# Last-batch tokens by one-hot products, a weight split by way of PSUM, and bound scatters, in a clustered attention and mixture-of-experts kernel

## The chip, the core and the metric

The kernel runs on one core of a Trainium2 chip. A core has five engines with queues of their own: PE (TensorE) for matrix products, DVE (VectorE) and ACT (ScalarE) for elementwise work, POOL (GpSimd) for elementwise work on SBUF and for DMAs with computed row numbers, and SP (SyncE), which issues the other DMAs. Each engine works its queue in order. The metric is the device time of one execution in microseconds; the median of three runs is quoted, and single executions of this kernel lie between 809 and 814 us.

## The reference

There are two parts. The first is attention over 4 batches of 8 heads, 768 tokens, 64 features, masked by clusters: a query sees only the keys that are assigned to its own centroid.

```python
q_assign = argmax(einsum('bhsd,hcd->bhsc', q_n, c_n), -1)
k_assign = argmax(einsum('bhsd,hcd->bhsc', k_n, c_n), -1)
mask = q_assign[:, :, :, None] == k_assign[:, :, None, :]
scores = where(mask, scale * (q @ k.T), -1e9)
attn = softmax(scores); out = attn @ v
```

Its output, seen as 3072 tokens of 512 features, goes through a two-stage router (4 groups, then 4 experts of the group), and each token through its one expert:

```python
h = maximum(xg[mask_e] @ w1[g, e], 0.0)      # 512 -> 1024
ye = h @ w2[g, e]                            # 1024 -> 512
out[tok_idx] = (g_w * e_w)[:, None] * ye
```

All is FP32. The kernel keeps that accuracy by splitting each operand into a high and a low FP16 part and adding three products (high by high, high by low, low by high).

## The kernel before, in words

**Attention.** The loop in `attention` goes through 32 heads of nine *steps*; a step is one 512-column piece of fine scores. In a step PE makes the fine scores (L342, L343, two PSUM buffers `psf`), ACT the exponentials (L347), POOL the low part of the probabilities (L349; in the last two heads DVE does every second one), PE the products with V of five steps earlier (L366, L367), and, up to 18 steps ahead, the coarse scores (L302), whose row maxima DVE takes out of PSUM (L305). `beside` runs at the end of each step and starts what is due: jobs at a given step, and *turns*, of which one at most starts in a step, the lowest priority number first. What shares the two PSUM buffers `psm` takes turns. The splits of later q, k and v already go by way of PSUM (`halves`, L198 and L199): ACT writes a scaled half there, and DVE subtracts the high part from it.

The instructions are not queued in the order of the code. A scheduler with a time model of its own fixes the order for each engine: an instruction may be placed early, into a gap, where the model has its inputs ready, and the order in the code is only a priority. `tc.issue_after(x)` forbids what is written under it to stand ahead of `x` on `x`'s own engine.

**Router.** After every second head `logits` adds a quarter of a batch's router products. `decide` then finds group and expert of each of the batch's 768 tokens, and a slot in a table in DRAM: one row of token number and gate for each expert and slot. Six scatters from POOL (L668, 128 rows each) write a batch's rows. For the last batch `decide` runs after attention, with `early` set.

**The first expert.** After batch 2 (of 0 to 3) `first` (L772) picks the expert with most tokens so far, f0. It loads f0's w1 in four chunks (`load_chunk`, 512 KB each, into the four buffers of `stage`), splits them (`split_chunk`: ACT the high part, L758, DVE the low part with one operation on two SBUF operands, L761), waits for batch 2's scatters, reads f0's table rows (L809), loads the chunks of w2, gathers up to 288 of f0's tokens (L889) and transposes them into `xTA`.

**After attention.** `part_a` puts those 288 tokens through f0; it also splits w2 there, between the first four of the eight pieces of the first layer (`up`, L927 to L930). Beside it the last batch is decided and scattered. f0's tokens of the last batch have an own region of the table, up to 128 rows. `slots_b` reads that region (`tB`) and the start of all regions (`tb`); `slots_b2` turns `tB` into row numbers (L1002) and gathers the rows (`xB`); `slots` brings `tb` into the order in which the experts are worked, by small FP32 products with a permutation (L1073), and gathers the rows of the first of them; `tokens` transposes `xB` on PE (L899, L901). `SLB`, `SLOTS` and `SLT` give the points of `part_a` behind which these are written. Then `ranks` works f0's last tokens (k = -1) and the other 15 experts (k = 0 to 14), with their weights streamed through `stage`, 4 MB each, and the results scattered to the output (L988).

## Time and profile before

| | |
|---|---|
| median of the runs (lowest to highest) | 810.94 us (809.08 to 813.51) |
| time of the profiled execution | 810.6 us |
| its span, first to last instruction | 808.9 us |
| busy: PE, DVE, ACT, POOL | 738.6, 621.1, 460.0, 497.0 us |
| mean granted clock of PE | 0.963 |
| attention | to about 441 us |
| part A, last batch's decision, f0's last tokens | 441 to 493 us |
| the other experts | 493 to 795 us |

A row of a timeline gives start and duration in us, engine, line, operation, and the tile written and those read; in brackets is the idle time of the engine just before, and what ended it. A row of groups gives the count, the busy time in all, the mean duration in ns, and the idle time before them. A row of stages gives the length of the stretch, the busy time of each engine with the number of its instructions, the clock that PE was granted, the share of DMA and GB/s.

### The profile page before, as it was taken

Reading aid. Unit: us, or ns where it says so; the run is one execution under the profiler, and the core shown is the slowest. Engines: PE = TensorE matmul, PEld = TensorE weight load, DVE = VectorE, ACT = ScalarE, POOL = GpSimd, SP = SyncE. Lnnn points to the kernel's source line nnn. Section 1 sums busy time; section 2 is a strip of 40 time slices with the busy share of each in tenths; the row PEclk is TensorE's granted clock in tenths of the full one; section 3 lists DMA queues with packets and bytes.
Section 4 is the critical chain, followed back from the end, with each engine's and each line's share of the span. In section 5 each row is a group of like instructions: output and inputs, shape, how many; then the busy total and the mean of one; then the engine's idle time right before and its main releaser. Section 6 shows DMA issues by size and latency. Waiting matters only on the chain. (4 is left out here: it accounts for less than half of the span.)

```text
span 808.9 us, 26554 instructions
## 1 busy us (share of the span) xinstructions
PE 738.6 (91%) x11034; PEld 627.1 (78%) x11034; DVE 621.1 (77%) x1193; ACT 460.0 (57%) x893; POOL 497.0 (61%) x497
## 2 busy tenths in 40 slices
PE   5899999989999899997699868999999999999992
PEld 3677788768887688875588655788779999999991
DVE  6998879878798788988865645767589988887840
ACT  4567868658686587765366445435544454555431
POOL 9487787697877878769663424525556544654330
PEclk6899999999999999999799989999999999999996
DMA  8856435235343352223210287866687678888700
GB/s 235 210 155 154 127 100 163 77 90 146 103 138 101 90 144 67 68 74 106 92 41 4 80 296 254 260 215 216 220 262 246 225 246 261 263 274 270 234 30 18
DMA packets 80616, 128.54 MB, mean 159 GB/s; under 512 B 9011, under 2 KB 47411, under 8 KB 80488
## 3 DMA queue, kind: packets, MB, share of 16 engines
q1 hardware_dynamic: 74636, 113.12, 46.8%
q0 software_dynamic: 5696, 13.61, 4.7%
q8 instruction: 88, 1.44, 0.8%
q14 instruction: 40, 0.33, 0.1%
q10 hardware_dynamic: 156, 0.03, 0.0%
HBM read 93.47 MB, written 14.11 MB: 133 GB/s over the span
## 5 line engine op out<-in xcount | busy, mean ns | idle before, releaser
L349 POOL TENSOR_TENSOR pl<-p 128x512 f16<-128x512 f32 x278 | 288.6, 1054 | 98.2 <-ACT p L347 93.8
L305 DVE TENSOR_REDUCE mpart<-psc 128x1 f32<-128x512 f32 (+1 forms) x282 | 190.3, 684 | 47.1 <-PE psc L302 46.6
L347 ACT ACTIVATE p<-psf 128x512 f32<-128x512 f32 x288 | 169.3, 595 | 80.3 <-PE psf L343 72.2
L366 PE MATMUL pso<-V,pl 128*128 128x65 f16 x1152 | 164.0, 195 | 5.5 <-POOL pl L349 5.3
L366 PE MATMUL pso<-V,p 128*128 128x65 f16 x1152 | 164.6, 195 | 0.8 <-issue 0.6
L367 PE MATMUL pso<-V,p 128*128 128x64 f16 x1152 | 163.7, 193 | 0.0
L367 PE MATMUL pso<-V,pl 128*128 128x64 f16 x1152 | 163.7, 192 | 0.0
L342 PE MATMUL psf<-A 82*128 82x384 f16 (+2 forms) x576 | 144.9, 277 | 2.3 <-DMA A<-mr 0.9
L343 PE MATMUL psf<-B 128*128 128x384 f16 (+2 forms) x576 | 145.1, 277 | 0.0
L367 PEld LDWEIGHTS <-p 128*128 128x128 bf16 x1152 | 113.6, 99 | 22.2 <-issue 1.5
L366 PEld LDWEIGHTS <-p 128*128 128x128 bf16 x1152 | 113.2, 98 | 16.8 <-issue 8.9
L302 PE MATMUL psc<-A 80*128 80x512 f16 (+1 forms) x376 | 109.7, 333 | 15.7 <-DVE mpart L305 14.4
L366 PEld LDWEIGHTS <-pl 128*128 128x128 f16 x1152 | 112.3, 97 | 6.5 <-POOL pl L349 5.9
L367 PEld LDWEIGHTS <-pl 128*128 128x128 f16 x1152 | 113.8, 99 | 0.6 <-issue 0.3
L930 DVE SCALAR_TENSOR_TENSOR hl<-psh,hh 128x160 f16<-128x160 f32 (+14 forms) x136 | 50.1, 370 | 56.4 <-ACT hh L929 47.2
L929 ACT ACTIVATE hh<-psh 128x160 f16<-128x160 f32 (+14 forms) x136 | 46.1, 346 | 64.8 <-PE psh L927 63.7
L927 PE MATMUL psh<-xT,wh0a 128*128 128x288 f16 (+7 forms) x512 | 75.6, 256 | 0.9 <-issue 0.5
L988 POOL DMA_INDIRECT out_dram<-y,ri x32 | 38.9, 1215 | 60.3 <-ACT y L987 55.2
L927 PE MATMUL psh<-xT,wh0b 128*128 128x272 f16 (+6 forms) x448 | 65.2, 254 | 1.6 <-ACT xT L901 1.2
L343 PEld LDWEIGHTS <-B 128*128 128x128 f16 x576 | 56.9, 99 | 11.2 <-issue 3.0
L342 PEld LDWEIGHTS <-A 82*128 82x128 f16 x576 | 55.9, 98 | 12.3 <-DMA A<-mr 1.0
L927 PE MATMUL psh<-xT,wl0a 128*128 128x288 f16 (+7 forms) x256 | 64.4, 256 | 1.0 <-issue 1.0
(297 smaller groups left out, 1747.5 us busy)
## 6 DMA issues: line engine op xcount, KB each, us to landing
st<-w SPq DMA_DIRECT2D x128, 512.0 KB
B<-parts SPq DMA_DIRECT2D x64, 192.0 KB
kx<-kT SPq DMA_DIRECT2D x16, 384.0 KB
qx<-qT SPq DMA_DIRECT2D x16, 384.0 KB
vx<-vr SPq DMA_DIRECT2D x16, 384.0 KB
A<-parts SPq DMA_DIRECT2D x32, 192.0 KB
xbuf<-xs SPq DMA_DIRECT2D x4, 1536.0 KB
A<-mk SPq DMA_DIRECT2D x56, 24.0 KB
```

Source lines behind the costliest of these rows:

```text
L302: last["mm"] = nc.tensor.matmul(out=pc[:, off:off + k1 - k0], lhsT=QA[h % 8][0:80, c * P:(c + 1) * P], rhs=KA[h % 8][0:80, k0:k1], start=T ...
L305: nc.vector.tensor_reduce(out=(mp[:, 0, 0:1], mp[:, :, 1], mp[:, 1, 0:1])[i], in_=pc.rearrange("p (a x) -> p a x", a=n), axis=AX.X, op=ALU ...
L342: nc.tensor.matmul(out=o, lhsT=KA[h % 8][0:82, ks], rhs=QA[h % 8][0:82, q0:q1], start=True, stop=False)
L343: nc.tensor.matmul(out=o, lhsT=KBs[h][:, ks], rhs=QBs[h][:, q0:q1], start=False, stop=True)
L347: cfg["exp"] = nc.scalar.activation(out=p32, in_=pf, func=AF.Exp, scale=QK / (SQ * SQ))
L349: (nc.vector if u in (EARLY if h < 2 else DVE_LO[h % 8] if h < NH - 2 else DVE_END) else nc.gpsimd).tensor_tensor(out=pl, in0=p32, in1=ph, ...
L366: nc.tensor.matmul(out=O[:, col:col + 65], lhsT=p[:, bs], rhs=vh, start=c == 0 and q == 0 and i == 0, stop=False, skip_group_check=True)
L367: nc.tensor.matmul(out=O[:, col:col + 64], lhsT=p[:, bs], rhs=vl, start=False, stop=c == NCH - 1 and i == 1, skip_group_check=True)
L927: self.mm = nc.tensor.matmul(out=ph[:, 0:M], lhsT=w[:, k, fs], rhs=xT[:, a, k], start=i == 0, stop=i == 3 * KD - 1)
L929: nc.scalar.activation(out=hh[:, f], in_=ph[:, 0:M], func=AF.Relu)
L930: self.ev = nc.vector.scalar_tensor_tensor(out=hl[:, f], in0=ph[:, 0:M], scalar=0.0, in1=hh[:, f], op0=ALU.max, op1=ALU.subtract)
L988: d = nc.gpsimd.indirect_dma_start(out=self.out, out_offset=bass.IndirectOffsetOnAxis(ap=idc, axis=0), in_=y[0:n], in_offset=None, bounds_ ...
```

## The change

Five things are changed.

1. `split_beside` takes the place of `split_chunk` for f0's weights. ACT writes the high part as before; then, in two turns of a `psm` buffer, ACT writes a scaled half of the chunk (512 columns) into PSUM, and DVE subtracts the high part from it.
2. w2 of f0 is loaded and split in `first`, thus in attention, and no longer in `part_a`. The four loads stand together ahead of the table read. `FIRST`, the number of steps between chunks, is 2 instead of 4. The two tiles of split w2 come from the pool `wa`.
3. A scatter of batches 0 to 2 and the gathers of `first` are bound behind POOL's latest low part by `issue_after`.
4. f0's tokens of the last batch are not read back from DRAM. `slots_b` compares each token's slot with the slot numbers of f0's last region and so makes one-hot matrices, 128 tokens by 128 slots for each of six token tiles, in FP32 (in a buffer of `stage`) and in FP16. `tokens_b` multiplies the last batch's attention output, which is still in SBUF, by them: 2 parts x 4 feature blocks x 6 tiles = 48 products of 128 columns give the transposed tokens at once, and six FP32 products of 2 columns give token numbers and gates. `tB`, `slots_b2` and that gather are gone.
5. `SLOTS` is 11 and `SLT` 13, counted in a `part_a` of 16 pieces (8 of the first layer, 8 of the second); before it was 18 and 17 of 20.

```diff
-FIRST = 4
+FIRST = 2
...
+        if lo.ins.engine == ET.Pool:
+            cfg["lo"] = lo
...
-            d = self.last["p"] = nc.gpsimd.indirect_dma_start(
+            with self.tc.issue_after(self.cfg["lo"].ins) if self.apart and not early and "lo" in self.cfg else ExitStack():
+                d = self.last["p"] = nc.gpsimd.indirect_dma_start(
...
-    SLOTS = 18
-    SLB = 11
-    SLT = 17
+    SLOTS = 11
+    SLT = 13
...
+    def after(self):
+        return self.tc.issue_after(self.cfg["exp"].ins) if "exp" in self.cfg else ExitStack()
+
+    def split_beside(self, st, hi, lo, i, q):
+        nc = self.nc
+        h, l = (w[:, *self.part(i, q)] for w in (hi, lo))
+        with self.after():
+            nc.scalar.activation(out=h, in_=st, func=AF.Copy, scale=WS)
+        n = st.shape[1] // 2
+        for j in range(2):
+            yield PSM, 1, 1
+            rows = slice(j * n, j * n + n)
+            t = self.R.psm.tile([P, 512], F32, name="psm").rearrange("p (a b) -> p a b", a=n)
+            with self.after():
+                nc.scalar.activation(out=t, in_=st[:, rows], func=AF.Copy, scale=WS)
+            nc.vector.tensor_tensor(out=l[:, rows], in0=t, in1=h[:, rows], op=ALU.subtract)
...
             if q >= 2:
-                with after():
-                    self.split_chunk(chunks[q - 2], *self.WA, 0, q - 2, 0)
+                yield from self.split_beside(chunks[q - 2], *self.WA, 0, q - 2)
...
+        w2A = [self.load_chunk(1, self.f0, q) for q in range(4)]
+        self.WA += self.wtiles(self.wa, 1)
         while R.done < R.B - 2:
             yield
...
-            self.w2A.append(self.load_chunk(1, self.f0, t + 1))
...
             if rows:
-                self.gather(ids[0:n, t:t + 1], n, xgs[t], rows)
-            for _ in range(4):
-                yield
+                with self.tc.issue_after(self.cfg["lo"].ins) if "lo" in self.cfg else ExitStack():
+                    self.gather(ids[0:n, t:t + 1], n, xgs[t], rows)
+            yield from self.split_beside(w2A[t], *self.WA[2:4], 1, t)
+        for q in range(nt, 4):
+            yield from self.split_beside(w2A[q], *self.WA[2:4], 1, q)
...
     def part_a(self):
-        w2 = self.W[1][0]
-        self.WA += w2
-        run = self.ffn(self.xTA, self.CA, self.WA, *self.colsA)
-        for q in range(4):
-            next(run)
-            yield
-            with self.tc.issue_after(self.R.last["v"].ins), self.tc.issue_after(self.R.last["a"].ins):
-                self.split_chunk(self.w2A[q], *w2, 1, q, 0)
-            yield
-        yield from run
+        yield from self.ffn(self.xTA, self.CA, self.WA, *self.colsA)
...
     def slots_b(self):
-        tB = self.small("tB", [P, 2])
-        R.reads(nc.sync.dma_start(out=tB, in_=R.table[E * R.BS:E * R.BS + P]))
...
+        nc.gpsimd.iota(sl, [[1, P]], base=E * R.BS, channel_multiplier=0, allow_small_or_imprecise_dtypes=True)
...
+        for c in range(T):
+            nc.vector.tensor_scalar(out=o32[:, c], in0=sl, scalar1=R.rows[:, c:c + 1], scalar2=None, op0=ALU.is_equal)
+        nc.scalar.copy(out=self.o16, in_=o32)
...
-    def slots_b2(self):
-        with self.tc.issue_after(self.ev.ins):
-            self.idB, self.gB = self.columns([self.tB[:, 0:1], self.tB[:, 1:2]], [P, 1], "b")
-        self.xB = self.gather(self.idB, P)
+    def tokens_b(self):
...
+        for a in range(2):
+            ps = R.psm.tile([P, 512], F32, name="psm")
+            for k in range(R.KD):
+                for c in range(T):
+                    nc.tensor.matmul(out=ps[:, k * P:(k + 1) * P], lhsT=xs[:, c, a, k * P:(k + 1) * P], rhs=self.o16[:, c], start=c == 0, stop=c == T - 1)
+            (nc.scalar.copy if a else nc.vector.tensor_copy)(out=xT[:, a], in_=ps.rearrange("p (k x) -> p k x", x=P))
+        ps = R.psm.tile([P, 512], F32, name="psm")
+        for c in range(T):
+            nc.tensor.matmul(out=ps[:, 0:2], lhsT=self.o32[:, c], rhs=self.pb[:, c], start=c == 0, stop=c == T - 1)
...
-            if i == X.SLB:
-                X.slots_b2()
             if i == X.SLOTS:
                 X.slots()
             if i == X.SLT:
-                X.xTB = X.tokens([X.xB], P)
+                X.xTB = X.tokens_b()
```

More of the change, by code (lines that the diff above doesn't have):

```diff
@@ L348, in fine @@
         ph = p32.bitcast(BF16)[:, 1::2]
-        (nc.vector if u in (EARLY if h < 2 else DVE_LO[h % 8] if h < NH - 2 else DVE_END) else nc.gpsimd).tensor_tensor(out=pl, in0=p32, in1=ph, op=ALU.subtract)
+        lo = (nc.vector if u in (EARLY if h < 2 else DVE_LO[h % 8] if h < NH - 2 else DVE_END) else nc.gpsimd).tensor_tensor(out=pl, in0=p32, in1=ph, op=ALU.subtract)
+        if lo.ins.engine == ET.Pool:
+            cfg["lo"] = lo
         Ph[h, u], Pl[h, u] = ph, pl
@@ L487, in av_next @@
             last = b == B - 1 and hh == H - 1
+            if last:
+                cfg["xs"] = XSt[b]
             if hh == H - 1:
@@ L526, in __init__ @@
         self.sm = ctx.enter_context(tc.tile_pool(name="rsm", bufs=1))
-        self.ident = cfg["ident"]
+        self.ident, self.cfg = cfg["ident"], cfg
         KD = self.KD = wr.shape[1]
@@ L655, in decide @@
         nc.vector.tensor_tensor(out=ps, in0=ps, in1=oe.rearrange("p t g x -> p t (g x)"), op=ALU.mult)
-        ds_ = sm.tile([P, T], F32, name="rds")
+        ds_ = self.rows = sm.tile([P, T], F32, name="rds")
         nc.vector.tensor_reduce(out=ds_, in_=ps, axis=AX.X, op=ALU.add)
@@ L667, in decide @@
                 yield
-            d = self.last["p"] = nc.gpsimd.indirect_dma_start(
-                out=self.table, out_offset=bass.IndirectOffsetOnAxis(ap=di[:, c:c + 1], axis=0),
-                in_=self.pay[:, t0 + c], in_offset=None)
+            with self.tc.issue_after(self.cfg["lo"].ins) if self.apart and not early and "lo" in self.cfg else ExitStack():
+                d = self.last["p"] = nc.gpsimd.indirect_dma_start(
+                    out=self.table, out_offset=bass.IndirectOffsetOnAxis(ap=di[:, c:c + 1], axis=0),
+                    in_=self.pay[:, t0 + c], in_offset=None)
             if self.apart:
@@ L789, in first @@
         self.WA = self.wtiles(self.wa, 0)
-        after = lambda: self.tc.issue_after(self.cfg["exp"].ins) if "exp" in self.cfg else ExitStack()
         chunks = []
@@ L809, in first @@
             R.reads(nc.sync.dma_start(out=tab[0:n, t], in_=tv[t * P:t * P + n]))
-        self.w2A = [self.load_chunk(1, self.f0, 0)]
-        for _ in range(FIRST):
+        for _ in range(FIRST + 1):
             yield
@@ L833, in first @@
             yield PSM, 2, 2
-            with after():
+            with self.after():
                 self.transposed(self.xTA, xgs[t], t, n, R.psm.tile([P, 512], F32, name="psm"))
@@ L843, in open @@
         wp = ctx.enter_context(tc.tile_pool(name="wp", bufs=1))
-        self.W = [[self.wtiles(wp, i, n) for n in "ab"] for i in range(2)]
+        self.W = [[self.wtiles(wp, 0, n) for n in "ab"], [self.WA[2:4], self.wtiles(wp, 1, "b")]]
         self.xp = ctx.enter_context(tc.tile_pool(name="mxp", bufs=2))
@@ L1053, in slots_b @@
         nc, R, E = self.nc, self.R, self.R.E
-        tB = self.small("tB", [P, 2])
-        R.reads(nc.sync.dma_start(out=tB, in_=R.table[E * R.BS:E * R.BS + P]))
-        self.tB = tB
+        T = R.rows.shape[1]
+        sl = self.small("sl", [P, P])
+        nc.gpsimd.iota(sl, [[1, P]], base=E * R.BS, channel_multiplier=0, allow_small_or_imprecise_dtypes=True)
+        t0 = R.N // P - T
+        pb = self.small("pb", [P, T, 2])
+        nc.vector.tensor_scalar(out=pb[:, :, 0], in0=R.pay[:, t0:t0 + T, 0], scalar1=-float(R.N), scalar2=None, op0=ALU.add)
+        nc.vector.tensor_copy(out=pb[:, :, 1], in_=R.pay[:, t0:t0 + T, 1])
+        o32 = self.stage.tile([P, 2, 512], F32, name="st").rearrange("p a b -> p (a b)")[:, 0:T * P].rearrange("p (c x) -> p c x", x=P)
+        self.o16 = self.small("o16", [P, T, P], F16)
+        for c in range(T):
+            nc.vector.tensor_scalar(out=o32[:, c], in0=sl, scalar1=R.rows[:, c:c + 1], scalar2=None, op0=ALU.is_equal)
+        nc.scalar.copy(out=self.o16, in_=o32)
+        self.o32, self.pb = o32, pb
         nt = self.nt = -(-max(self.caps) // P)
@@ L1059, in slots_b @@
         R.reads(nc.sync.dma_start(out=self.tb, in_=R.table.rearrange("(e s) w -> e s w", s=R.BS)[0:E, 0:nt * P]))
-    def slots_b2(self):
-        with self.tc.issue_after(self.ev.ins):
-            self.idB, self.gB = self.columns([self.tB[:, 0:1], self.tB[:, 1:2]], [P, 1], "b")
-        self.xB = self.gather(self.idB, P)
+    def tokens_b(self):
+        nc, R = self.nc, self.R
+        T = R.rows.shape[1]
+        xs = self.cfg["xs"]
+        xT = self.xp.tile([P, 2, R.KD, P], F16, name="xT")
+        for a in range(2):
[7 more added lines that the diff above has]
+            nc.tensor.matmul(out=ps[:, 0:2], lhsT=self.o32[:, c], rhs=self.pb[:, c], start=c == 0, stop=c == T - 1)
+        self.idB = self.small("bi", [P, 1], I32)
+        self.gB = self.small("bg", [P, 1])
+        nc.vector.tensor_scalar(out=self.idB, in0=ps[:, 0:1], scalar1=float(R.N), scalar2=None, op0=ALU.add)
+        nc.vector.tensor_scalar(out=self.gB, in0=ps[:, 1:2], scalar1=1.0 / (XS * WS * WS), scalar2=None, op0=ALU.mult)
+        return xT
     def slots(self):
```

## The prediction

> **What bounds the kernel now.** I read the stages first: PE's busy time and granted clock in stretches of the span.
>
> ```profile
> core 0: us, PE busy (x) PEld busy (x) DVE busy (x) ACT busy (x) POOL busy (x), PEclk, DMA share, GB/s
> 300.00:340.00 40.00, 39.73 (x775) 33.15 (x775) 33.58 (x72) 28.27 (x57) 31.80 (x32) 1.00 0.25 62
> 380.00:400.00 20.00, 12.58 (x208) 10.06 (x205) 17.05 (x21) 8.65 (x15) 15.30 (x15) 0.83 0.27 81
> 400.00:420.00 20.00, 16.98 (x285) 13.80 (x285) 15.84 (x27) 10.13 (x18) 12.43 (x13) 0.83 0.18 55
> 440.00:460.00 20.00, 17.61 (x208) 13.46 (x206) 14.96 (x50) 9.01 (x17) 7.04 (x6) 1.00 0.23 81
> 460.00:480.00 20.00, 13.22 (x92) 9.95 (x92) 5.84 (x11) 5.91 (x9) 3.52 (x5) 0.83 0.68 237
> 480.00:500.00 20.00, 16.41 (x187) 12.42 (x186) 10.31 (x21) 12.77 (x24) 13.62 (x12) 0.91 0.79 271
> 500.00:600.00 100.00, 100.00 (x864) 78.50 (x863) 73.63 (x112) 44.25 (x82) 44.71 (x36) 1.00 0.72 229
> ```
>
> PE is the bound nearly everywhere (39.73 of 40 us in steady attention, 100 of 100 in the ranks). So time is to be had only where PE stands still: 10.4 us in 380 to 420, and 2.4 + 6.8 + 3.6 = 12.8 us in 440 to 500. The other experts' stage has no idle PE; whatever comes earlier ahead of it, comes off the end.
>
> The first hole, from the timeline (start, duration) and windows of 5 us:
>
> ```profile
> 375.56 9.02 POOL L349 TENSOR_TENSOR pl<-p 128x512 f16<-128x512 f32 x9
> 379.14 6.52 DVE L761 SCALAR_TENSOR_TENSOR wl<-st,wh 128x1024 f16<-128x1024 f32 x1
> 386.78 0.58 PE L302 MATMUL psc<-A 80*128 80x256 f16 x2 [5.49 <-DVE mpart L305]
> 402.92 0.58 PE L302 MATMUL psc<-A 80*128 80x512 f16 x1 [4.85 <-DVE mpart L305]
> 451.19 1.23 DVE L761 SCALAR_TENSOR_TENSOR wl1a<-st,wh1a 128x1024 f16<-128x1024 f32 x1
> 451.44 1.88 POOL L668 DMA_INDIRECT table<-pay,rdi  x1 [12.07 <-DVE rdi L659]
> 385.00:390.00 5.00, 3.22 (x37) 2.47 (x37) 3.89 (x13) 0.82 (x2) 1.20 (x2) 0.51 0.35 105
> 400.00:405.00 5.00, 2.08 (x21) 1.56 (x21) 4.70 (x7) 0.00 (x0) 1.17 (x2) 0.52 0.31 95
> 405.00:410.00 5.00, 5.00 (x82) 4.13 (x80) 3.69 (x4) 3.48 (x6) 2.92 (x3) 0.80 0.04 13
> L761 DVE SCALAR_TENSOR_TENSOR wl<-st,wh 128x1024 f16<-128x1024 f32 x4 | 15.8, 3938 | 0.8 <-ACT wh L758 0.7
> ```
>
> The low part of a weight chunk takes DVE 1.23 us where POOL is in DMA work (451), and 6.52 us where POOL runs nine low parts in a row: that one ends at 385.66, about 1.1 us after POOL's row of 375.56 + 9.02 = 384.58. DVE waits for POOL here; behind it wait the row maxima, and behind these PE, 5.49 and 4.85 us. Then PE runs at half clock for a while: 3.22 x 0.49 + 2.08 x 0.48 + 5.00 x 0.20 = 3.6 us more.
>
> **The change, part by part.** (1) *Splits of w1.* DVE's one operation with two SBUF operands becomes two subtractions whose first operand ACT has put into PSUM. The kernel has such pairs already, 384 columns wide:
>
> ```profile
> L199 DVE TENSOR_TENSOR parts<-psm,parts x48: 543/551/559, 61.8 to 334.5; 128x384 f16<-128x384 f32 x48
> L198 ACT ACTIVATE psm<-vx 128x384 f32<-128x384 f32 x24 | 11.8, 490 | 3.9 <-DVE V L199 3.9
> L347 ACT ACTIVATE p<-psf 128x512 f32<-128x512 f32 x288 | 169.3, 595 | 80.3 <-PE psf L343 72.2 <-PE psc L302 6.6
> L758 ACT ACTIVATE wh<-st 128x1024 f16<-128x1024 f32 x4 | 4.2, 1056 | 0.0
> ```
>
> The first row decides: 48 subtractions with a PSUM operand, in attention beside a POOL that is 80% busy, none over 559 ns. So the holes of 10.4 us and the 3.6 us of slow clock behind them should go: **-14.0**. (The Trainium skill, SBUF — State Buffer, Who interferes with whom, says that of a DVE operation with two SBUF inputs and a GpSimd operation that reads SBUF the later one waits until the first finishes. By that rule a split loses at most one POOL operation, about 1 us, so the four would give 4 and not 14; the trace has a wait behind several in a row and 5.49 us on PE, and the trace decides.)
>
> At 512 columns a subtraction takes at most 551 x 512 / 384 = 735 ns, so DVE pays 8 x 0.7 = 5.9 us for w1 where it paid 15.8. It stays below PE.
>
> (2) *Splits of w2, moved from the first expert's products into attention.* Each split costs ACT 1.06 + 2 x 0.60 = 2.25 us. New on ACT are four high parts and 16 copies: 4 x 1.06 + 16 x 0.60 = 13.8 us; new on DVE for w2 5.9. Following the loop's turns in the code, one step being one 512-column piece of the fine scores: w1 falls on steps 243 to 261, w2 on 266 to 277 (scores end at 287). ACT over the 19 steps of w1: 19 x 0.60 + 4 x 2.25 + two router copies of 768 columns, between the 512 and the 1024 column rows, at 0.8 + two finishing casts of 384 columns at 0.49 = 23.0, and small ones; PE has, by 31 such pieces in its 40 us of steady attention less the q, k and v work that has ended, about 1.2 us a step: 23. Over w2's 12 steps: 7.2 + 9.0 + 1.6 + 0.5 = 18.3, while PE, whose coarse scores end at step 269, has about 4 x 1.2 + 8 x 1.0 = 13. ACT is the later one there by some 5, less one step that two score buffers cover. With 0.1 to 0.2 us of bank exchange a piece (3.9 us of idle in 24 pieces of the L198 row, and others have less) I take **+6.5**. Bounds: 0 if ACT's idle time takes all of it, +13.8 if all of it lies on the path. The w2 loads go to SP four at a time at step 263, behind w1's last split and ahead of the table read; a chunk has 3 steps before its split, and SP's next row-maximum transfer has 6 before its use: nothing, up to +2.
>
> (3) *Scatters of batches 0 to 2, and the first gathers, bound behind POOL's latest low part.*
>
> ```profile
> 163.55 1.20 POOL L668 DMA_INDIRECT table<-pay,rdi  x1 [0.33 <-DMA qx<-qT]
> ...
> 173.02 0.96 POOL L668 DMA_INDIRECT table<-pay,rdi  x1 [0.30 <-issue]
> PE pso L366 <- POOL pl L349: 2.5, 2, 2.2
> PE pso L366 <- POOL pl L349: 2.8, 2, 2.2
> 370.57 1.63 DVE L786 TENSOR_TENSOR cb<-cb,ft 128x16 f32<-128x16 f32 x1
> ```
>
> Six scatters stand in 10.5 us of POOL with only three low parts between them, so they were issued far ahead of their place in the code (every 5 steps, 4 for batch 2): 7.3 us of scatters in 8 to 9 steps, and PE waits 2.5 us (140 to 200) and 2.8 (245 to 300). Spread over 25 steps POOL, with 1.05 of about 1.3 us, works most of that off between them; I leave 0.4 each: **-4.5**. In batch 2 the crowded POOL also holds up small DVE operations (1.63 us for 16 columns); I count **-1**. Bounds 0 to -7.5. The price: batch 2's last scatter stands at step 262 and no longer ahead of it, so the table read of the first expert comes up to 15 steps later; its ids are wanted at 266 and may keep DVE waiting for 1 us, its rows at 279, which leaves a dozen us. The transposes fall on 279, 283, 286 (now 281, 286, 289), so part A isn't later: nothing, up to +2.
>
> (4) *The end of attention.* Waits of PE from 440 to 505, then the timeline:
>
> ```profile
> PE psm L899 <- DMA xg<-xbuf,bi: 4.6, 1, 4.6
> ...
> PE psh L927 <- DVE hl L930: 1.8, 2, 1.3
> PE psm L899 <- DMA xg<-xbuf,ri: 1.0, 1, 1.0
> 441.62 0.41 PE L927 MATMUL psh<-xTA,wh 128*128 128x288 f16 x2
> 459.44 0.96 POOL L668 DMA_INDIRECT table<-pay,rdi  x1 [0.30 <-issue]
> 465.89 0.15 DVE L1002 CAST bi<-tB 128x1 int32<-128x1 f32 x1 [5.32 <-DMA tB<-table]
> 466.53 1.14 PE L945 MATMUL psy<-hh,wh1a 128*128 128x288 f16 x8 [2.07 <-DVE yl L949]
> 466.93 0.99 POOL L889 DMA_INDIRECT xg<-xbuf,bi  x1 [4.39 <-issue]
> 474.21 1.03 PE L899 MATMUL psm<-ident,xg 128*128 128x128 f16 x8 [4.58 <-DMA xg<-xbuf,bi]
> 478.05 1.85 PE L1073 MATMUL psm<-perm,tb 16*128 16x16 f32 x12
> 493.25 0.41 PE L927 MATMUL psh<-xT,wh0a 128*128 128x288 f16 x2 [0.51 <-issue]
> ```
>
> The last batch's tokens go scatter, table, DVE, gather (7.3 us from 466.93 to PE), transposes. With the one-hot products the waits of 4.6 and of 2.1 (DVE stuck on the table) go, the rank's gather wait of 1.0 and the 1.3 on hl too, the latter since four wl1a of 1.23 leave DVE: 9.0. The slow clock goes: 13.22 x 0.17 + 16.41 x 0.09 = 3.7. Added on PE: 48 products of 128 columns at 0.06 (eight such take 1.03 at half clock) 2.7, six of FP32 at 0.15 (twelve in 1.85) 0.9, less eight transposes 0.5: +3.1. DVE's six comparisons of 128 columns (above the 0.15 of one column, below the 0.55 of 384) and ACT's 768-column copy lie beside part A's products, the slot numbers in POOL's 12.07 us of idle before its first scatter. One wait can take the old one's place: the expert permutation now comes after the second of four output blocks. PE gets there about 441.6 + 11.7 (96 of 0.122, by eight in 1.14) + 5.9 + 2 router + 1 = 462; scatters without DVE's four splits end near 458.5 instead of 460.4, and the table lands 5.5 us after that as now (460.4 to 465.9), at 464: 2 us, bounds 0 to 6. Sum -9.0 - 3.7 + 3.1 + 2 = **-7.6**, bounds -13 to 0. The rank's rows then have till 485 to arrive; gathered from 467 on, with the 7.3 us of the crowded one, they are there at 478. One of four staging buffers is held by the one-hot until then: covered by the five others.
>
> Sum: -14.0 + 6.5 - 5.5 - 7.6 = -20.6. From the profiled execution's 810.6 us (span 808.9, 1.7 around it) that is **790 us**; the median shown, 810.9, is 0.3 above that execution.
>
> **The rivals.**
> *ACT has room and PE finds the table there.* The L347 row's 80 us of idle ACT speaks for it, the count of step 266 to 277 against. The 6.5 falls to 1 and the 2 to 0, the scatters give all 7.5: 781.
> *The permutation waits like the old gather.* The weight stream starts ahead of the table read or the scatters stay slow; PE stands 6 us or more and slows its clock: (4) gives nothing, 798. For it: tokens were placed before their data now, too (4.58 us). (The Trainium skill, TensorE: Matmul & The Clock Gate, What's actually happening, has the clock fall to half after an idle window of about 3.4 us; the 0.51 after the 5.49 us wait agrees, and a 6 us wait would bring it again.)
> *The splits don't do what they say:* the new subtractions wait for POOL as the old did. Then -14 is lost: 804. The 559 ns maximum speaks against.
> *Slower: ACT and the two psm banks.* In the crowded steps each of the 24 pieces holds back the next exponential for its length and a wait for its bank, which DVE frees only after row maxima that wait for PE. Break-even is 20.6 + 6.5 = 27 us over eight splits, 3.4 us a split, 1.1 above its 2.25. At 4.4 a split: 35, so 819. For it: ACT falls behind PE at w2's steps. Against: 0.16 us of wait a piece in the L198 row.
>
> **How the numbers follow.** Forecast 790 (784 to 796): 0.53. 781: 0.15. 798: 0.17. 804: 0.03. Both the 798 case and all of ACT's 13.8 on the path, 805 to 812: 0.05. 819: 0.07. Under 0.5% (4 us) this kernel's change can't be told from none. Faster is the first four, 0.88; same 0.05; slower 0.07. From 777 to 805 the range leaves out the last two and a little below.
>
> **What would show it.** L761 in attention gone, no PE wait over 2 us on mpart, clock 1.0 from 380 to 420 (else 1 is wrong). Steps 266 to 277 with ACT near full and PE waiting on p (2). No wait of PE on pl near 170 and 270 (3). No PE wait on a gather for B, one under 3 us at the permutation, rank 0's first product 7 to 8 us sooner after part A's start than 51.6 (4). An unchanged ranks stage. A time over 805 would say that ACT, or the wait at the permutation, took what DVE gave.

## The result, and the profile after

The changed kernel takes 783.26 us (median; 782.34 to 784.30), the kernel before 810.91 us (809.08 to 813.51): a ratio of 0.9657, 95% interval 0.9628 to 0.9686. The forecast was 790 us, in a range of 777 to 805. The profiled execution after took 782.34 us, with a span of 780.6 us (before 808.9) at a mean granted clock of 0.978 (before 0.963). Two executions in the series below took far longer than all others of their kernel (2536.98 us of the kernel before, 1047.63 us of binding and split together), and the ratios leave them out.

The stages after, with the columns of the prediction's first fence:

```profile
380.00:400.00 20.00, 18.94 (x352) 15.49 (x350) 16.22 (x40) 16.07 (x30) 19.23 (x20) 1.00 0.25 68
400.00:420.00 20.00, 19.20 (x417) 16.93 (x415) 14.18 (x29) 17.21 (x33) 9.86 (x10) 1.00 0.05 16
440.00:460.00 20.00, 17.95 (x157) 14.44 (x157) 7.59 (x13) 5.71 (x8) 7.32 (x7) 0.91 0.74 247
460.00:480.00 20.00, 19.20 (x216) 14.74 (x214) 12.40 (x22) 14.66 (x28) 7.57 (x7) 1.00 0.82 280
480.00:500.00 20.00, 20.00 (x180) 16.17 (x178) 17.25 (x22) 8.93 (x19) 11.41 (x9) 1.00 0.83 258
```

PE is busy 38.1 of the 40 us from 380 to 420, where it had 29.6 at a clock of 0.83, and the clock there is now 1.00. ACT, 8.65 and 10.13 before, stands at 16.07 and 17.21 of 20.

The new splits on DVE and ACT (count, then shortest, median and longest in ns, first and last start), and the waits of PE from 140 to 200 us:

```profile
L784 DVE TENSOR_TENSOR wl<-psm,wh x16: 669/691/692, 366.2 to 408.9; 128x512 f16<-128x512 f32 x16
L783 ACT ACTIVATE psm<-st x16: 573/605/632, 365.6 to 408.2; 128x512 f32<-128x512 f32 x16
```

```profile
PE psm L651 <- DVE roe L639: 1.3, 1, 1.3
PE psc L302 <- DVE mpart L305: 0.2, 1, 0.2
```

Sixteen subtractions from PSUM, none over 692 ns, stand in place of eight operations on two SBUF operands, of which one took 6.52 us. And the wait of PE on `pl`, 2.5 us before, is gone. The timeline of POOL beside it, and then that of the end of attention (PE and SP's queue):

```profile
168.00 1.19 POOL L674 DMA_INDIRECT table<-pay,rdi  x1 [0.18 <-issue]
169.22 5.02 POOL L349 TENSOR_TENSOR pl<-p 128x512 f16<-128x512 f32 x5
174.41 0.99 POOL L674 DMA_INDIRECT table<-pay,rdi  x1 [0.17 <-issue]
...
421.10 0.41 PE L950 MATMUL psh<-xTA,wh 128*128 128x288 f16 x2
435.83 0.01 SPq L756 DMA_DIRECT2D st<-w  x1
437.52 0.96 POOL L674 DMA_INDIRECT table<-pay,rdi  x1 [0.30 <-issue]
443.92 0.35 SPq L1084 DMA_DIRECT2D tb<-table  x1
445.98 1.23 PE L1114 MATMUL psm<-perm,tb 16*128 16x16 f32 x9 [1.65 <-DMA tb<-table]
469.66 0.41 PE L950 MATMUL psh<-xT,wh0a 128*128 128x288 f16 x2
487.45 0.53 PE L950 MATMUL psh<-xT,wh0b 128*128 128x272 f16 x2
```

A scatter now comes every 6 to 7 us with five low parts between. Part A begins at 421.10 where it began at 441.62, which is 20.5 us earlier. Rank 1's first product comes at 487.45 where it came at 513.93, 26.5 us earlier; the remaining 1.8 of the span's 28.3 us lie in the ranks, where the profiles of this study differ by 3 us among themselves (292.7 to 295.9).

**Where the time came from.** The time at which a head is finished is the start of DVE's row that takes its denominators out of PSUM. After:

```profile
354.69 0.15 DVE L382 TENSOR_SCALAR DEN<-pso 128x6 f32<-128x6 f32 x1
392.21 0.16 DVE L382 TENSOR_SCALAR DEN<-pso 128x6 f32<-128x6 f32 x1
421.30 0.17 DVE L382 TENSOR_SCALAR DEN<-pso 128x6 f32<-128x6 f32 x1 [1.63 <-PE pso L369]
```

These are heads 25, 28 and 31; before, the same rows stood at 364.67, 414.70 and 441.81. The table gives, for every profile of this study, how much later (+) or earlier (-) than before each stage was passed, and last how long it takes from part A's first product to rank 1's. Heads 9 to 25 hold the scatters of batches 0 and 1, heads 25 to 28 w1's splits and the scatters of batch 2, heads 28 to 31 w2's splits where attention has them. What lies ahead of head 9 is start-up, which differs from execution to execution; it is in no stage.

| kernel | to head 9 | 9 to 25 | 25 to 28 | 28 to 31 | A to rank 1 |
|---|---|---|---|---|---|
| before | 0 | 0 | 0 | 0 | 72.31 |
| changed | -0.12 | -9.86 | -12.51 | +1.98 | 66.35 |
| changed, second profile | -0.36 | -10.02 | -13.80 | +2.76 | 68.38 |
| before, scatters bound | +0.43 | -9.94 | -3.92 | +1.32 | 72.05 |
| before, w1 split by PSUM | +0.35 | -1.28 | -10.30 | 0.00 | 68.23 |
| before, both of these | +2.37 | -9.96 | -13.79 | +2.95 | 67.36 |
| changed, scatters not bound | +2.87 | +1.86 | -9.80 | +0.75 | 67.02 |
| changed, split in SBUF | +0.32 | -9.96 | -10.77 | +4.91 | 66.88 |
| changed, scatters one step apart | +0.11 | -5.85 | -13.35 | +2.75 | 68.16 |
| changed, w2 split in part A | -0.54 | -9.99 | -12.53 | +0.04 | 71.03 |
| changed, table and gather | +0.27 | -9.86 | -13.66 | +2.99 | 69.87 |
| changed, w2's copies by VectorE | +0.27 | -10.02 | -13.75 | +5.50 | 64.91 |
| changed, permutation a step later | +1.26 | -10.05 | -13.61 | +2.76 | 65.72 |
| changed, w2's splits later | -0.33 | -10.03 | -13.72 | +2.49 | 66.35 |

### The profile page after: what moved, and what is told of

The parts are those of the page before. It is cut to its first block, busy times and chain, and to the rows that moved or that the text cites. A ratio compares the mean times of both kernels' runs of the same rounds, so it can differ in the third digit from the quotient of the medians.

```text
span 780.6 us, 26678 instructions
## 1 busy us (share of the span) xinstructions
PE 733.3 (94%) x11086; PEld 626.5 (80%) x11086; DVE 612.0 (78%) x1209; ACT 466.8 (60%) x910; POOL 495.6 (63%) x497
## 3 DMA queue, kind: packets, MB, share of 16 engines
q0 software_dynamic: 5616, 13.35, 4.9%
## 5 line engine op out<-in xcount | busy, mean ns | idle before, releaser
L368 PE MATMUL pso<-V,p 128*128 128x65 f16 x1152 | 161.6, 193 | 0.0
L368 PE MATMUL pso<-V,pl 128*128 128x65 f16 x1152 | 161.2, 194 | 0.0
L369 PE MATMUL pso<-V,pl 128*128 128x64 f16 x1152 | 161.0, 191 | 0.0
L369 PE MATMUL pso<-V,p 128*128 128x64 f16 x1152 | 160.8, 191 | 0.0
L952 ACT ACTIVATE hh<-psh 128x160 f16<-128x160 f32 (+14 forms) x136 | 46.6, 347 | 65.7 <-PE psh L950 64.3
L912 POOL DMA_INDIRECT xg<-xbuf,ri x32 | 43.5, 1359 | 39.8 <-PE psm L922 25.7
```

Of the source, the lines that this page charges most:

```text
L368: nc.tensor.matmul(out=O[:, col:col + 65], lhsT=p[:, bs], rhs=vh, start=c == 0 and q == 0 and i == 0, stop=False, skip_group_check=True)
L369: nc.tensor.matmul(out=O[:, col:col + 64], lhsT=p[:, bs], rhs=vl, start=False, stop=c == NCH - 1 and i == 1, skip_group_check=True)
L912: self.got = nc.gpsimd.indirect_dma_start(out=xg[0:n].rearrange("p a d -> p (a d)"), out_offset=None, in_offset=bass.IndirectOffsetOnAxis( ...
L952: nc.scalar.activation(out=hh[:, f], in_=ph[:, 0:M], func=AF.Relu)
```

## The experiments

The theory after the two traces: the scatters are worth about 10 us and not 5.5, because each wait on `pl` is followed by half clock, and the splits less than 14. The rivals are the prediction's own terms. "Before" and "changed" are the two kernels of this case; ratios are to the kernel before, run on the same chip (medians of 810.50, 807.58 and 809.15 us there), and the changed kernel has 0.9657 and, a second time, 0.9715. The same kernel's ratio thus moved by 0.6%, some 5 us, from one series to another; smaller differences between series are read from the stages.

### Binding alone, and the changed kernel without it

The kernel before, with only this (`lo` is kept as in the changed kernel):

```diff
-            d = self.last["p"] = nc.gpsimd.indirect_dma_start(
+            with self.tc.issue_after(self.cfg["lo"].ins) if self.apart and not early and "lo" in self.cfg else ExitStack():
+                d = self.last["p"] = nc.gpsimd.indirect_dma_start(
```

> The kernel before, with its scatters of batches 0 to 2 bound behind POOL's latest low part and nothing else changed. Theory A (the binding is worth what heads 10 to 19 show between the two traces, 5.1 + 4.7 us, because each crowd of scatters costs PE its wait and as much again at half clock; and DVE's long waits at the w1 splits come from POOL's backlog behind batch 2's scatters, so they shrink to about one POOL operation): 811 - 10 - (8 to 12) = 789 to 793, no PE wait over 2 us on the row maxima. Theory B (the binding is worth 10, but DVE's split waits as long as POOL has any low part to run, crowd or not): 801, with both PE waits of about 5 us still there. The prediction's own term (no slow clock): 805.5.

Measured: 796.97 us (796.26 to 799.12), ratio 0.9835 (0.9817 to 0.9852): 13.4 us from one small edit, between the two expectations and far over the prediction's term. Batches 0 and 1 gave 9.9 us; another 3.9 came in heads 25 to 28, where DVE still splits in SBUF. DVE and POOL there, then PE's waits from 360 to 415 us:

```profile
383.21 5.02 DVE L765 SCALAR_TENSOR_TENSOR wl<-st,wh 128x1024 f16<-128x1024 f32 x1 [0.73 <-issue]
383.11 4.02 POOL L349 TENSOR_TENSOR pl<-p 128x512 f16<-128x512 f32 x4
387.30 1.78 POOL L672 DMA_INDIRECT table<-pay,rdi  x1 [0.17 <-issue]
```

```profile
PE psc L302 <- DVE mpart L305: 7.6, 3, 3.9
```

In the kernel before, from 360 to 425 us:

```profile
PE psc L302 <- DVE mpart L305: 12.8, 4, 5.5
```

POOL's rows are four low parts long instead of nine, and DVE's operation still waits for a whole row: begun at 383.21 beside a row that ends at 387.13, it ends at 388.23. So binding also shortens PE's waits behind the splits, from 12.8 us in four to 7.6 in three, of which 3.9 is the longest. Neither theory's sign came: one wanted no wait over 2 us, the other both waits of about 5.

The other way round, the changed kernel with the scatters as before:

```diff
-            with self.tc.issue_after(self.cfg["lo"].ins) if self.apart and not early and "lo" in self.cfg else ExitStack():
-                d = self.last["p"] = nc.gpsimd.indirect_dma_start(
+            d = self.last["p"] = nc.gpsimd.indirect_dma_start(
```

> The changed kernel with its scatters free to be placed early again; the gathers stay bound. The binding as the two traces show it: 783.3 + 10 = 793, PE waiting on pl 2 to 3 us near 170 and 270 and at half clock after it. The prediction's term: 783.3 + 5.5 = 789. If the scatters only matter together with the old splits: 783.

Measured: 798.64 us (793.87 to 801.97), ratio 0.9839 (0.9800 to 0.9878), slower than all three expectations. Its profile spent 3 us more on start-up than that of the changed kernel; the stages say 11.7 us in heads 9 to 25 and 2.7 in heads 25 to 28. PE's waits from 140 to 200 us in it, and the stages behind them:

```profile
PE pso L368 <- POOL pl L349: 2.8, 2, 2.2
```

```profile
176.00:178.00 2.00, 0.03 (x1) 0.03 (x2) 1.32 (x3) 0.94 (x2) 1.97 (x3) 0.90 0.03 3
178.00:180.00 2.00, 2.00 (x20) 1.46 (x21) 0.00 (x0) 0.25 (x1) 2.00 (x3) 0.50 0.00 0
180.00:182.00 2.00, 2.00 (x48) 1.72 (x47) 1.21 (x2) 0.98 (x2) 2.00 (x3) 0.50 0.00 1
182.00:184.00 2.00, 2.00 (x30) 1.63 (x27) 1.48 (x3) 1.57 (x3) 1.93 (x3) 0.50 0.03 8
```

The wait of 2.2 us is followed by six us at half clock, which are 3 us more. In the kernel before the same wait was followed by less: by the rows of 174 to 180 us shown at the end, 0.88 x 0.28 + 2.00 x 0.50 + 2.00 x 0.08 = 1.4 us more. This slow clock is what the prediction's term left out; that it is longer in this run is why heads 9 to 25 are even 1.86 us slower than in the kernel before.

### How the scatters are spread

The changed kernel, with a scatter of batches 0 and 1 every step instead of every five:

```diff
-            for _ in range(1 if early else 4 if then else 5):
+            for _ in range(1 if early else 4 if then else 1):
```

> The changed kernel (783.3 us), with the six scatters of each of batches 0 and 1 one step of the router apart where it has five; each stays bound behind a low part of GpSimd. Theory A: what cost the time in the kernel before is that low parts of later heads stand behind a row of scatters; then the waits of TensorE on the low part (2.2 to 2.9 us) and the half clock behind them return: +8 to +10 us for the two batches, 791 to 794 us. Theory B: a scatter that is bound behind a low part lets one low part through each time, at any spacing; then no wait on a low part over 1 us, and 782 to 785 us.

Measured: 787.06 us (784.35 to 788.43), ratio 0.9729 (0.9701 to 0.9758). Neither was right by its time: heads 9 to 25 won 5.85 us instead of 9.9. Theory B's sign, no wait over 1 us, did come. POOL's timeline and PE's waits from 160 to 190 us:

```profile
166.11 0.99 POOL L674 DMA_INDIRECT table<-pay,rdi  x1 [0.18 <-issue]
167.12 1.06 POOL L349 TENSOR_TENSOR pl<-p 128x512 f16<-128x512 f32 x1
168.34 0.99 POOL L674 DMA_INDIRECT table<-pay,rdi  x1 [0.17 <-issue]
```

```profile
PE pso L368 <- POOL pl L349: 1.5, 2, 0.9
```

Bound, the scatters take turns with the low parts, and no wait is over 0.9 us; behind such waits the clock stayed at 1.00 (all windows from 168 to 182 us). So binding alone takes the long wait and the half clock away, about 6 us of the 10; five steps between give the other 4.

### The splits: alone, with the binding, and without PSUM

The kernel before with w1 through `split_beside`:

```diff
-                with after():
-                    self.split_chunk(chunks[q - 2], *self.WA, 0, q - 2, 0)
-            for _ in range(FIRST):
+                yield from self.split_beside(chunks[q - 2], *self.WA, 0, q - 2)
+            for _ in range(2):
```

> The kernel before (810.9 us), with only the split of the first expert's w1 by way of PSUM; w2 is split after attention, the scatters are not bound, the gather stays. The prediction's term: the holes are VectorE's alone, 14.0 us: 797 us. Rival, from the runs with the parts undone: most of the holes come from GpSimd's low parts being late behind the scatters, and with the scatters unbound the low parts stay late whatever the split does; the parts but for the binding were worth 12.3 us together, 7.8 of it behind attention: 804 to 808 us, with TensorE still waiting on the low part of the softmax near 170 and 270 us.

Measured: 794.63 us (793.77 to 795.08), ratio 0.9836 (0.9812 to 0.9860): 13 us, near the prediction's term, and the rival fell. But only 10.3 us of it lie in heads 25 to 28, where the splits are; from part A to rank 1 there are 4.1, and in heads 9 to 25 1.3, though no line was changed in either. PE still waits 3.1 and 3.0 us on `pl` near 170 and 270, as expected without the binding; behind batch 1's wait the clock stayed at 1.00 here (the rows are at the end), which is about the 1.3 us. The rival had read too much out of the run without binding: heads 25 to 28 won 9.80 us there, too.

Binding and split together, in the kernel before:

> The kernel before (810.9 us), with the scatters bound and the split of w1 by way of PSUM together; w2's split and the last batch's tokens as before. Each alone gave 13 us (ratios 0.9835 and 0.9836). Theory A: the two are independent: ratio 0.967, 784 us. Theory B: they share a part, since a binding that keeps GpSimd's low parts in time also shortens VectorE's holes: the split is worth 5 to 8 us beside the binding: 789 to 792 us.

Measured: 786.50 us (785.19 to 787.28), ratio 0.9729 (0.9679 to 0.9779), between the two, and the interval holds both. The stages decide it: heads 9 to 25 gave 9.96 us, all of the binding, and heads 25 to 28 13.79, which is the 3.92 of the binding and 9.87 of the split, as against 10.30 alone. Up to head 28 the two add up, so theory B fell; what lacks at the end is 2.4 us of start-up in this profile and 2.95 us in heads 28 to 31, where PE waits 1.6 us on `p` and 1.0 on `pl`. From part A to rank 1 it won 5.0 us, with the code of the kernel before. On the same chip the changed kernel took 784.90 us (0.9715): binding and the split of w1 are nearly all of the gain, and what w2's move, the one-hot products and the new points add to them, some 2 us, cannot be told from none.

The changed kernel, with the low part of each chunk in one operation on two SBUF operands, at the same place:

```diff
-        n = st.shape[1] // 2
+        nc.vector.scalar_tensor_tensor(out=l, in0=st, scalar=WS, in1=h, op0=ALU.mult, op1=ALU.subtract)
         for j in range(2):
             yield PSM, 1, 1
-            rows = slice(j * n, j * n + n)
-            t = self.R.psm.tile([P, 512], F32, name="psm").rearrange("p (a b) -> p a b", a=n)
-            with self.after():
-                nc.scalar.activation(out=t, in_=st[:, rows], func=AF.Copy, scale=WS)
-            nc.vector.tensor_tensor(out=l[:, rows], in0=t, in1=h[:, rows], op=ALU.subtract)
```

> The changed kernel, but the low part of each chunk of the first expert made by one DVE operation on two SBUF operands as before; the 16 copies into PSUM are left out, their turns stay. Theory A (DVE's long wait needs a POOL that is behind): 781 to 787, each of the eight operations at 1.2 to 2.3 us. Theory B (DVE waits for as long as low parts follow one another on POOL): the four of w1 wait 4 to 6 us again and PE behind them, 795 or more.

Measured: 791.12 us (788.36 to 799.99), ratio 0.9802 (0.9734 to 0.9871), a wide interval, but above the changed kernel in every run. In its timeline (DVE, POOL and PE) there are two holes of PE:

```profile
371.05 4.44 DVE L777 SCALAR_TENSOR_TENSOR wl<-st,wh 128x1024 f16<-128x1024 f32 x1
370.37 4.02 POOL L349 TENSOR_TENSOR pl<-p 128x512 f16<-128x512 f32 x4
397.65 0.15 DVE L833 CAST idA<-tabA 128x1 int32<-128x1 f32 x1 [1.79 <-DMA tabA<-table]
398.98 1.20 DVE L777 SCALAR_TENSOR_TENSOR wl<-st,wh 128x1024 f16<-128x1024 f32 x1
401.30 0.38 PE L302 MATMUL psc<-A 80*128 80x512 f16 x1 [2.71 <-DVE mpart L305]
```

Of eight operations one met a row of low parts and took 4.44 us; the others took 1.20 to 1.72. The second hole is another thing: DVE stands on the table read for f0's token numbers, 1.79 and then 0.81 us, with the row maxima behind it. So of what this kernel loses only some 2 to 3 us (heads 25 to 28: -10.77 against -12.51 and -13.80) are the SBUF operands. The same kind of operation cost far more in the run with binding alone. What differs there is its place among the low parts: further apart, and each bound behind an exponential. An operation that began ahead of a low part took no longer than alone (366.08 us, 1.23 us); the one that began inside the row did. How much of the split's 10 us is PSUM and how much is place, these runs do not separate.

The operand rule itself was looked at with the eight `psm` copies of w2 made by DVE, which then read one operand in SBUF:

```diff
-            with self.after():
-                nc.scalar.activation(out=t, in_=st[:, rows], func=AF.Copy, scale=WS)
+            if i:
+                nc.vector.tensor_scalar(out=t, in0=st[:, rows], scalar1=WS, scalar2=None, op0=ALU.mult)
+            else:
+                with self.after():
+                    nc.scalar.activation(out=t, in_=st[:, rows], func=AF.Copy, scale=WS)
```

> The changed kernel, with the eight copies of w2's chunks into PSUM (128x512, 0.605 us each on ScalarE) made by VectorE instead, from one operand in SBUF. Theory A: VectorE waits for GpSimd only where it reads two operands in SBUF; the copies take 0.6 to 0.8 us each, ScalarE gets 4.8 us back, and heads 29 and 30 win 1 to 2 us: 781 to 783 us. Theory B: a copy from SBUF waits for GpSimd's operation as the two-operand split did (3 to 6 us where low parts run in a row): 786 to 791 us.

Measured: 783.93 us (783.26 to 785.23), ratio 0.9707 (0.9681 to 0.9732). Its groups from 340 to 430 us, and PE's waits there:

```profile
L783 DVE TENSOR_SCALAR psm<-st 128x512 f32<-128x512 f32 x8 | 5.3, 679 | 0.0
```

```profile
PE psf L342 <- ACT p L347: 3.0, 2, 1.8
```

679 ns each: no wait behind POOL. Theory A's mechanism held and its gain did not come: heads 28 to 31 lost 5.5 us instead of 2.0 to 2.8. The copies now stand in DVE's queue, and PE waits on `p` all the same.

### The end of attention

The changed kernel with the last batch's tokens by table and gather, as before (`tB` and `slots_b2` back, its columns at step 7 of part A, `SLOTS` 14):

```diff
-                X.xTB = X.tokens_b()
+                X.xTB = X.tokens([X.xB], P)
```

> The changed kernel, with the last batch's tokens of the first expert read from the table and gathered again as in the kernel before, the index columns made at step 7 of part A, the permutation at step 14. The prediction's term for this part (7.6 us): 791 us, with TensorE waiting over 4 us on the gather. The two traces (the way from the last head to rank 1 became 6.0 us shorter, and 1.8 us of what the ranks gained has nothing to do with it): 788 to 790 us. Rival: the products' own 3.1 us and the wait at the permutation eat most of it: 784 to 786 us.

Measured: 786.31 us (785.94 to 786.80), ratio 0.9733 (0.9710 to 0.9756): by its time at the rival's end. But this chip is 3 us faster with the kernel before, and by its ratio the time is 0.9733 x 810.9 = 789 us, where the traces had it (the changed kernel's two ratios give 783 and 788). So the stages have to say it. PE's waits from 421 to 500 us and a stage of it:

```profile
PE psy L968 <- DVE yl L972: 5.0, 1, 5.0
PE psm L922 <- DMA xg<-xbuf,bi: 2.2, 1, 2.2
```

```profile
440.00:460.00 20.00, 12.77 (x68) 8.80 (x66) 5.31 (x9) 5.30 (x7) 2.94 (x2) 0.71 0.67 230
```

The waits that the prediction named come back, 7.2 us with a slow clock, and yet the way from part A to rank 1 is only 3.5 us longer than in the changed kernel's first profile and 1.5 than in its second.

The changed kernel with w2 split in part A again, a chunk behind each of its first four turns:

```diff
-            yield from self.split_beside(w2A[t], *self.WA[2:4], 1, t)
...
+            for _ in range(4):
+                yield
...
+            with self.tc.issue_after(self.R.last["v"].ins), self.tc.issue_after(self.R.last["a"].ins):
+                self.split_chunk(self.w2A[q], *self.WA[2:4], 1, q, 0)
```

> The changed kernel with w2 of the first expert split after attention again, in the first four pieces of the first layer, high part on ACT and low part in one DVE operation; its loads stay early. The prediction's term (ACT costs 6.5 us in attention) with 1 to 2 us back at the end: 778. The heads' times in the two traces (0.9 us lost at head 26, 2.0 at heads 29 and 30): attention 2 us shorter, and 2 to 4 us lost at the end, since the four operations of 1.23 us stand between the scatters and the router again: 783 to 785.

Measured: 784.59 us (782.97 to 785.61), ratio 0.9684 (0.9661 to 0.9708), as the heads' times had it. Heads 28 to 31 lose nothing (+0.04), so w2's splits cost attention 1.9 to 2.7 us (by the changed kernel's two profiles); and part A takes it back, 71.03 us to rank 1. PE's waits from 418 to 470 us:

```profile
PE psh L949 <- DVE hl L952: 4.4, 2, 4.0
```

### Two versions beside the changed kernel

On one chip: the changed kernel again, one with the permutation a step later, and one with that and with w2's splits spread further.

> The changed kernel once more, so that the two versions of this series have it on the same chip: ratio 0.966, 783 us.

Measured: 784.90 us (783.31 to 786.61, six runs), ratio 0.9715 (0.9683 to 0.9747). In its profile the permutation does not wait 1.65 us, but (timeline, then a window):

```profile
445.99 1.25 PE L1114 MATMUL psm<-perm,tb 16*128 16x16 f32 x5 [4.55 <-DMA tb<-table]
```

```profile
445.00:450.00 5.00, 4.01 (x18) 3.50 (x19) 1.23 (x4) 1.06 (x1) 0.15 (x1) 0.50 0.98 336
```

Of the 2.9 us more, 2.0 are PE's own: it came to the permutation 21.25 us after part A's first product, where the first profile has 23.23, mostly because PE had waited only 0.3 us on `hh` ahead of it and not 2.1. The table came 0.9 us later (25.80 us after that product, for 24.88).

```diff
-    SLOTS = 11
+    SLOTS = 12
```

> The changed kernel, with the permutation of the table after step 12 of part A instead of 11, so that a step of products lies before its wait. Theory A: the wait of 1.65 us on the table read is gone and nothing takes its place: 1.6 us under the changed kernel. Theory B: the lists of the first ranks come a step (2.2 us) later, and rank 0's products wait on their gather: the same, or up to 1 us over it.

Measured: 783.90 us (782.13 to 789.29), ratio 0.9718 (0.9680 to 0.9756): no difference that can be told. The wait is still 2.6 us: the read is issued at 444.42 us here and ends the wait 2.8 us later, and the way to rank 1 is 65.7 us.

```diff
-            yield from self.split_beside(w2A[t], *self.WA[2:4], 1, t)
-        for q in range(nt, 4):
-            yield from self.split_beside(w2A[q], *self.WA[2:4], 1, q)
+            if t < 2:
+                yield from self.split_beside(w2A[t], *self.WA[2:4], 1, t)
+                yield
+        yield
...
                 self.transposed(self.xTA, xgs[t], t, n, R.psm.tile([P, 512], F32, name="psm"))
             yield
+            if t > 0:
+                yield from self.split_beside(w2A[t + 1], *self.WA[2:4], 1, t + 1)
```

> The changed kernel, with the permutation after step 12, and the splits of w2 further apart: two chunks with the gathers as now, one each after the second and third transposition of part A's tokens. Theory A: ScalarE's queue is shorter in heads 29 and 30, which were 2.0 us late behind it, and part A needs w2 only 17 us after its first product: 2 to 4 us under the changed kernel. Theory B: the last splits fall into the end of attention, where VectorE and ScalarE finish the last rows, and delay these by what was won: 0 to 2 us under it, no more than the permutation gives.

Measured: 781.11 us (780.64 to 783.15), ratio 0.9669 (0.9638 to 0.9700): each of its six runs is under each of the six of the changed kernel, by 3.8 us in the median, though the two intervals of the ratio still touch. The reason expected is not what did it: heads 28 to 31 lose 2.49 us against 2.76, while the way from part A to rank 1 is 66.35 against 68.38 us, with a wait of 3.3 at the permutation instead of 4.5. But 66.35 us is also what the changed kernel had in its first profile, so what makes this version faster is open.

## Why the prediction was right, step by step

The sign of each part held, and so did the mechanism of the splits and the scatters; the forecast was 7 us too high for 783.3. The four terms came out otherwise: three are off by about 4 us or more, and their errors go both ways, so that the total came so near is in part luck. By its number the rival of 781 (ACT has room and PE finds the table there) was nearer, but not by its parts: w2's splits cost 2.0 to 2.8 us and not 1, the permutation waited and the scatters gave 13.8 us and not 7.5. The rivals of 804 and 819 fell with the 692 ns and with these 2.0 to 2.8 us.

1. *Splits of w1, -14.0.* Alone the split gave 13 us in time; by the stage of the splits 10.3 without the binding and 9.9 with it. L761 is gone from attention, PE's waits on `mpart` are 0.7 us at most from 340 to 425, the clock is 1.00: all as named. The term counted the whole hole, and the hole was partly POOL's lateness: binding takes 3.9 us of it. The 4 us that the prediction worked out beside the Trainium skill's rule did not come true. That the operand in PSUM did all of it is not shown (the run with the split in SBUF).
2. *Splits of w2, +6.5.* Heads 28 to 31 took 2.0 and 2.8 us longer, nearly all of it w2's splits by the run with w2 in part A. ACT is near full from 400 to 420 as named, and PE waits on `p`, but little (changed kernel, 391 to 422 us):

```profile
PE psf L342 <- ACT p L347: 0.8, 3, 0.4
```

   The term that was mis-sized is the count of 18.3 us of ACT against 13 of PE; of its 5 us less than half came, and why is open. The move also paid in part A, under (4): with w2 split there, the one-hot products in place, the way to rank 1 is 71.0 us for 66.35 and 68.38.
3. *Bound scatters, -5.5.* This term was mis-sized most: 9.9 us for batches 0 and 1 and 3.9 for batch 2, 13.4 by time. It priced the wait on `pl` at its own 2.5 and 2.8 us, with 0.4 left of each. Nothing was left, and PE's idle time in heads 9 to 25 fell by 6.1 us, from 203.82 - 194.05 = 9.8 to 193.96 - 190.28 = 3.7, as against the 4.5 of the term. Behind each batch's wait stood half clock, about 1.5 us more a batch, which the same prediction had counted for the splits and the gather, and not here. For batch 2 it counted 1 us. Its bound of -7.5 did not hold it.
4. *End of attention, -7.6.* The two traces give 6.0 to rank 1, but only 1.5 to 3.5 are the one-hot products' by the run with table and gather. Rank 0's first product came 3.1 us sooner after part A's start (48.6 for 51.6), in the second profile 1.1, and not 7 to 8. The waits that the prediction named are gone: PE's idle time from part A to rank 0 fell from 51.63 - 39.91 = 11.7 to 48.56 - 42.85 = 5.7 us. But PE was busy 2.9 us more there, nearly the 3.1 of the sum, and other waits and the permutation's took part of the time. Part of what was booked here was no part of the gather: in the kernel before PE stood 2.0 us around 493 on nothing that the profile shows (waits of PE from 430 to 505 us):

```profile
PE psh L927 <- issue: 2.0, 3, 1.0
```

   In the run with binding and split, whose code is the same there, that wait is missing and the way to rank 1 is 67.4 us; with the split alone it is 68.2, with the binding alone 72.05. So the old code's way goes from 67.4 to 72.3 us, the changed kernel's 66.35 and 68.38 are not clear of it, and what this part gained is not shown. Why the old code's way differs so is open. The permutation, for which 2 us stood with bounds of 0 to 6, took 1.65 and 4.55: the table came 7.5 us after the last scatter (438.48 to 445.98), not the 5.5 that were carried over from before. In the second profile half clock follows it at once, as the rival of the permutation had it, at a smaller size. (In the sum of the added products 48 x 0.06 is 2.9 and not 2.7; nothing hangs on it.)

Summed for the changed kernel's profile: -9.9 (heads 9 to 25), -12.5 (25 to 28), +2.0 (28 to 31), -6.0 (to rank 1), -1.8 (ranks), -0.1 in start-up: -28.3 us of span, against -20.6. The scatters' surplus, 13.8 for 5.5, is about the whole difference of 7.7; the other errors nearly cancel, and nothing in the prediction's working made them do so.

## What to carry to other kernels

A wait in a row of waits is priced with the clock behind it, where a slow clock does follow: look at the windows of the clock after every wait that is to go, not only after the long ones. A hole that names one engine (DVE's row maxima here) can have its length from another's backlog (POOL behind scatters), so the edit that shortens the backlog takes a share of every hole that it feeds. And a DMA that is issued far ahead of its place in the code costs the queue it stands in; binding it behind an ordinary instruction of that engine was a few lines and half of the gain. Before a gain is booked to a new piece of code, look at how much the old piece's time differs between profiles: here by 5 us.

## What the runs showed of the hardware

A DVE operation on two SBUF operands that began inside a row of low parts on POOL waited to the row's end and ended 1.1 us after it (385.66 for 384.58, 388.23 for 387.13, 375.49 for 374.39): 6.52 us in a row of nine, 5.02 and 4.44 in rows of four. Where the next low part began 0.1 us after the end of the one before (409.16 and 409.06 in the kernel before), the operation got in between and took 2.03 us. It took 1.20 to 1.23 us where POOL was elsewhere or began second. In that case POOL waited: here two low parts took 2.59 us instead of 2.04 (the changed kernel with the split in SBUF).

```profile
366.08 1.23 DVE L777 SCALAR_TENSOR_TENSOR wl<-st,wh 128x1024 f16<-128x1024 f32 x1 [1.48 <-ACT wh L776]
366.61 2.59 POOL L349 TENSOR_TENSOR pl<-p 128x512 f16<-128x512 f32 x2 [1.50 <-ACT p L347]
```

With one SBUF operand, from SBUF to PSUM or from PSUM and SBUF, it took 0.68 and 0.69 us beside the same POOL. (The Trainium skill, SBUF — State Buffer, Who interferes with whom, says that two SBUF inputs contend with a GpSimd instruction that reads SBUF, and at most one, outside the 2-port modes, doesn't. The runs agree with that; they add that the wait lasted for as many instructions as followed one another without a gap.)

What followed a wait of PE was not the same each time. The wait of 2.2 us on `pl` was followed by three to six us at half clock for both batches in the kernel before and in the changed kernel with its scatters not bound, and for batch 0 in the run with the split alone; for batch 1 there the clock stayed at 1.00. A wait of 2.6 us (the split in SBUF, at 376 us) also left it at 1.00, one of 1.8 us (w2's copies by VectorE, at 409 us) was followed by half clock, and the waits of 0.9 us with the scatters one step apart were not. So these runs give no length of wait from which the clock falls. (The Trainium skill, TensorE: Matmul & The Clock Gate, What's actually happening, gives an idle window of about 3.4 us for the fall to half clock; here a wait of 2.2 us was enough five times in six, in stretches like that of 174 to 176 us before, in which PE was busy 0.88 of 2 us.)

The kernel before, then the split alone:

```profile
174.00:176.00 2.00, 0.88 (x15) 0.80 (x15) 0.56 (x1) 0.07 (x1) 1.99 (x2) 0.72 0.01 1
176.00:178.00 2.00, 2.00 (x19) 1.27 (x18) 0.32 (x1) 0.94 (x3) 2.00 (x3) 0.50 0.00 1
178.00:180.00 2.00, 2.00 (x57) 1.92 (x54) 1.45 (x4) 0.90 (x2) 2.00 (x3) 0.92 0.03 8
...
276.00:278.00 2.00, 0.60 (x15) 0.55 (x15) 0.65 (x2) 0.05 (x1) 1.97 (x3) 1.00 0.01 1
278.00:280.00 2.00, 2.00 (x53) 1.68 (x54) 0.88 (x2) 1.24 (x3) 2.00 (x3) 1.00 0.04 9
```

The table read for the permutation was issued 5.4 us after the last scatter had been issued in the changed kernel (438.48 to 443.92 us), behind a weight load on the same queue; the first table read of the kernel before was issued 2.75 us after it (460.40 to 463.15), with no such load just ahead. The same kernel waited for it 1.65 us in one execution and 4.55 in another; that the load delays the scatters' landing is argued from the order of the rows, and was not tried.
